# Three edits to the opening of a spectral filter with a low-rank mixer: order of table loads, packed f16 transposes, and the slots of one load

## The chip, the cores and the metric

The kernel runs on one core of one Trainium2 chip. The metric is the device time of one launch in microseconds (us), as the median of several runs. TensorE is called PE, VectorE DVE, ScalarE ACT, GpSimd POOL and SyncE SP, as in the profile; PEld is PE's weight load and a "q" behind an engine's name is its instruction queue.

## The reference

```python
X = np.fft.rfft(x, axis=1)                      # x: 8 x 3136 x 256, float32
Y = X * (filt_r + 1j * filt_i)[None]            # 1569 frequencies x 256
x = np.fft.irfft(Y, n=3136, axis=1)
h = x.transpose(0, 2, 1) @ U @ V                # U: 3136 x 32, V: 32 x 3136
u = x + h.transpose(0, 2, 1)
out = u + np.maximum(u @ w_ch1, 0) @ w_ch2      # w_ch1: 256 x 1024, w_ch2: 1024 x 256
```

Eight batches: a filter in the frequency domain along the sequence, a low-rank mixing along the sequence, and a two-layer network on each row.

## The kernel before

The Fourier transform of length 3136 is taken as 64 x 49, each half as matrix products. Frequencies come in 32 steps `s`. They are handled two at a time: index `m` runs from 0 to 15. Each step has its own table for the transform forward (`t2`) and back (`g12`), which are constants loaded from memory, and its own 256-wide rows of the filter (`ft`, real and imaginary). Tables and filter are loaded in four parts of eight steps, `PARTS = ((0, 8), (8, 16), (16, 24), (24, 32))`; in this text they are called part 0 to part 3, so part 1 covers `m` = 4 to 7. (The short name of the change counts from one.)

A part's filter is in use only after `swap_real` and `swap_imag` (DVE, lines 187 and 194) have copied it to the upper 64 partitions, the imaginary one with its sign turned.

Batch 0 goes a way of its own, without a round trip through memory:

- `first_f1` multiplies the four chunks of `x` with the 64-point matrix, one group of four rows `r0` after the other, and evicts the products in turns by ACT and DVE (L299, L301) into `at`. Matmuls named `keep` fill PE's gaps here. The loads of the tables are called from inside this loop. Each call first clears two columns of the destination on DVE (L156); the load on SP's queue (L157) waits for that, so a load leaves when DVE reaches the place in its order where the call stands.
- `first_a` (L321, L323) transposes two steps of `at` into the form in which the second transform reads them.
- `first_mid` is the loop over `m`. In turn `m` DVE multiplies spectrum and filter (`both_products`, L444, named `uv`), PE transforms the products of turn `m - 1` back (`back`, L340), the spectrum of turn `m + 2` forward (`forward`, L436, named `px`) and does one more `first_a`. ACT evicts what `back` gives (L343, named `et`). At the start of a new part DVE makes that part's swaps. Tables of parts 2 and 3 are called in turns `m` = 1 and 5. From turn 6 on, each turn takes one unit of batch 1's first transform (`fill`, from `f1_units`, L402 and L406/L408, named `pf` and `asb`), whose results go out to a buffer `c1` in memory (L412).
- Behind the loop stands the second turn of the data: 25 rows of `et`, each in two halves of 128 columns, are multiplied with the identity (L379, `pe`) and evicted to `e2` (L383 by ACT, L385 by DVE), two rows or 512 columns an eviction. `prep_u` (L263, L266, L268), three units of `fill` and one of `v_units` stand between them at fixed rows.
- Then `h1_unit(0)` (L503, L507) sums `e2` over the sequence, and the network's matmuls begin (L525, L530, L562, L584).

All other batches run interleaved with the network of the batch before, by an order written out by hand. A slot is half of a pair of matmul groups, 48 slots a batch; `put(slot, generator)` sets in which slot a step stands. `load_a` (L421) loads a quarter of the steps from `c1`, `stream` works on it (L436, L444 or L455/L457, L472, L476) and stores the result in `c2` (L478), and `load_e` (L428) reads it back turned. These three are issued from SP's queue, each waiting there for what it needs, so that one that waits holds up those behind it.

The pools decide little here: tag `m` has four PSUM banks of 2 KB a partition, tag `o` two, tag `a2` four buffers.

```python
for n0 in range(0, NH, 2):
    pt = bank("m", "pe")                  # 128 x 512 f32, one bank
    ...
    if n0 % 4:
        nc.scalar.copy(dst, pt[0:k, 0:w * DM])
    else:
        nc.vector.tensor_copy(dst, pt[0:k, 0:w * DM])
```

Of the kernel before, what the change touches and what calls it, by code (L numbers as in the profile page):

```python
# [9 lines left out]
F16 = mybir.dt.float16  # L10
# [6 lines left out]
DM = 256  # L17
RANK = 32
ESC = 16.0
NH = 25  # L20
# [66 lines left out]
def kernel(  # L87
# [11 lines left out]
    nc = tc.nc  # L99
# [5 lines left out]
    sel_d = nc.inline_tensor(sel_np, name="seld")  # L105
    t2_d = nc.inline_tensor(t2_np, name="t2d")
    g_d = nc.inline_tensor(g_np, name="gd")
# [6 lines left out]
    ps = ctx.enter_context(tc.tile_pool(name="ps", bufs=2, space=bass.MemoryType.PSUM))  # L114
    ctx.enter_context(tc.manual_schedule())
    BUFS = {"x": 1, "f": 1, "m": 4, "o": 2}

    def bank(tag, name):
        return ps.tile([128, 512], F32, tag=tag, bufs=BUFS[tag], name=name)
# [22 lines left out]
    idn = cst.tile([128, 128], F16)  # L142
    nc.sync.dma_start(idn, idn_d.ap())
    t2 = cst.tile([98, NS * 128], F16)
    g12 = cst.tile([128, NS * 2 * 98], F16)
    ft = cst.tile([128, 2 * NS * DM], F16)
    nyq = cst.tile([65, DM], F32)
    PARTS = ((0, 8), (8, 16), (16, 24), (24, 32))
# [1 line left out]
        for c in (0, NS * DM):  # L150
            nc.vector.memset(ft[32:64, c + a * DM:c + b * DM], 0.0)

    def load_tables(a, b):

        for dst, src, w in ((t2, t2_d, 128), (g12, g_d, 196)):
            nc.vector.memset(dst[:, a * w:a * w + 2], 0.0)  # L156
            nc.sync.dma_start(dst[:, a * w:b * w], src.ap()[:, a * w:b * w])  # L157

# [26 lines left out]
    def swap_real(a, b):  # L185

        nc.vector.tensor_copy(ft[64:128, a * DM:b * DM], ft[0:64, a * DM:b * DM])

    def swap_imag(a, b):

        fb = NS * DM
        if a == 0:
            nc.vector.memset(ft[0:1, fb:fb + DM], 0.0)
        nc.vector.tensor_scalar_mul(ft[64:128, fb + a * DM:fb + b * DM],
                                    ft[0:64, fb + a * DM:fb + b * DM], -1.0)
# [26 lines left out]
    sel = cst.tile([32, 128], F16)  # L222
# [52 lines left out]
    def first_f1():  # L275
        ne = 0
        keep = bank("x", "keep")
        xs = [st[0]["x"][c] for c in range(len(CH))]
        for r0 in range(0, NH - 1, 4):
            if r0 == 8:  # L280
                load_tables(*PARTS[0])
                nc.sync.dma_start(sel, sel_d.ap())
            if r0 == 20:
                load_tables(*PARTS[1])
            for dh in range(2):
                for k in range(4 if r0 < 16 else 0):
                    nc.tensor.matmul(keep[:, k * 128:(k + 1) * 128], w64[:, :], idn[:, :],
                                     start=True, stop=True, skip_group_check=True)
                pa = bank("m", "pa")
                for rr in range(4):  # L290
                    c = next(k for k in range(len(CH)) if r0 + rr < c0[k + 1])
                    o = (r0 + rr - c0[c]) * DM + dh * 128
                    nc.tensor.matmul(pa[:, rr * 128:(rr + 1) * 128], xs[c][:, o:o + 128], w64[:, :],
                                     start=True, stop=True, skip_group_check=True)
                for h in range(2):
                    dst = atv[:, dh, :, h * NH + r0:h * NH + r0 + 4]
                    src = pa.rearrange("p (r h k) -> p h k r", h=2, k=64)[:, h]
                    if ne % 2:
                        nc.vector.tensor_copy(dst, src)  # L299
                    else:  # L300
                        nc.scalar.copy(dst, src)  # L301
                    ne += 1
        pa = bank("m", "pa")
        o = (NH - 1 - c0[-2]) * DM
        for dh in range(2):
            nc.tensor.matmul(pa[:, dh * 64:(dh + 1) * 64],
                             xs[-1][0:64, o + dh * 128:o + (dh + 1) * 128], w64[0:64, 0:64],
                             start=True, stop=True, skip_group_check=True)
        nc.scalar.copy(atv[:, :, :, NH - 1],
                       pa[:, 0:128].rearrange("p (e k) -> p e k", e=2))  # L310
# [15 lines left out]
    def first_mid(fill):  # L326

        et = sb.tile([128, 2 * NH * 128], F16, tag="e2", bufs=2, name="et")
        etv = et.rearrange("p (e r h k) -> p h e r k", e=2, h=2, k=64)
        pend = None  # L330

        def back(m, uv):
            pi = bank("fx"[m % 2], "pi")
            for sl in range(2):
                for dh in range(2):
                    for fi in range(2):
                        g = (4 * m + 2 * sl + fi) * 98
                        o = fi * 512 + sl * DM + dh * 128
                        a = (dh * 2 + sl) * 98
                        nc.tensor.matmul(pi[:, a:a + 98], uv[:, o:o + 128], g12[:, g:g + 98],  # L340
                                         start=(fi == 0), stop=(fi == 1), skip_group_check=True)
            for h in range(2):
                nc.scalar.copy(  # L343
                    etv[:, h, :, 0:NH - h, 4 * m:4 * m + 4],
                    pi[:, 0:392].rearrange("p (e k r) -> p e r k", e=2, r=NR)
                    [:, :, h * NH:h * NH + NH - h])

        def ahead(m):
            return forward(m, st[0]["a"][m // 4], ("m",))

        pxs = [ahead(0), ahead(1)]
        for m in range(NS // 2):
            for k, part in enumerate(PARTS):
                if k and 2 * m == part[0]:
                    swap_real(*part)
                    swap_imag(*part)
            uv = both_products(m, pxs.pop(0))
            if pend is not None:
                back(*pend)
            pend = (m, uv)  # L360
            if m + 2 < NS // 2:
                pxs.append(ahead(m + 2))
            if m + 3 < NS // 2:
                first_a(m + 3)
            for k, part in enumerate(PARTS):
                if k > 1 and 2 * m + 14 == part[0]:
                    load_tables(*part)
            if m >= 6:
                next(fill)
        back(*pend)  # L370
        e2 = new_e2(0)
        for n0 in range(0, NH, 2):
            pt = bank("m", "pe")
            w = min(2, NH - n0)
            k = 64 if w == 1 else 128
            for rr in range(w):
                for dh in range(2):
                    o, a = rr * DM + dh * 128, (dh * NH + n0 + rr) * 128
                    nc.tensor.matmul(pt[0:k, o:o + 128], et[:, a:a + k], idn[:, :],  # L379
                                     start=True, stop=True, skip_group_check=True)  # L380
            dst = e2[0:k, n0 * DM:(n0 + w) * DM]
            if n0 % 4:
                nc.scalar.copy(dst, pt[0:k, 0:w * DM])  # L383
            else:
                nc.vector.tensor_copy(dst, pt[0:k, 0:w * DM])  # L385
            if n0 == 6:
                prep_u()
            if n0 in (10, 14, 18):
                next(fill)
            if n0 == 22:  # L390
                next(vgen)

    def f1_units(b, both):
# [37 lines left out]
    def forward(m, a2, xtags):  # L431
        ml = m % (KG // 2)
        px = bank(xtags[m % len(xtags)], "px")
        for sl in range(2):
            s = 2 * m + sl
            nc.tensor.matmul(px[:, sl * DM:(sl + 1) * DM], t2[:, s * 128:(s + 1) * 128],  # L436
                             a2[:, (2 * ml + sl) * DM:(2 * ml + sl + 1) * DM],
                             start=True, stop=True, skip_group_check=True)
        return px
# [54 lines left out]
    def one(load, b, k):  # L494
        load(b, k)
        yield
# [108 lines left out]
    def put(slot, gen):  # L605
        sched.setdefault(int(slot + 0.5), []).append(gen)
# [8 lines left out]
    SB = 48  # L615

    first_f1()
    swap_real(*PARTS[0])
    swap_imag(*PARTS[0])
    nc.vector.tensor_copy(ft[64:65, 0:DM], nyq[64:65, :])  # L620
    for m in range(3):
        first_a(m)
# [16 lines left out]
    for k, t in enumerate(steps):  # L639
        put(t, mid)  # L640
        b, m = divmod(k - LAG, NP)
        if k >= LAG and m % GP == GP - 1:
            put(t + (4 if b else 3), one(load_e, b + 1, m // GP))
    for b in range(1, nb):
        for gi in range(NS // KG):
            t = steps[NP * (b - 1) + GP * gi]
            put(t - (6 if b == 1 else 8), one(load_a, b, gi))
        put(SB * b - 4, h1_unit(b))
        if b > 1:
            fill = f1_units(b, b == 2)  # L650
            for k in range(NF):
                put(4 + 1.1 * k if b == 2 else steps[NP * (b - 1)] - 49 + 3 * k, fill)
            for c in range(len(CH)):
                if b > 2:
                    put(steps[NP * (b - 1)] - 68 + 10 * c, one(load_x, b, c))
# [53 lines left out]
```

## Time and profile before

| | |
|---|---|
| median of 3 runs | 558.92 us (558.39 to 560.25) |
| profiled execution | 560.77 us, span of its instructions 559.0 us |
| PE busy | 528.6 us, 95% of the span |
| DVE, ACT, POOL busy | 367.9, 363.6, 243.4 us |
| idle PE before 75 us | 21 us of the 75 |
| mean granted clock of PE | 0.989 |

The span is shorter than the time of its execution by 1.77 us, which lie ahead of the first and behind the last instruction. Rows of the timeline give the start, the duration, the engine with the line, and in brackets how long the engine had been idle and what ended that. Rows of the waits give the time in total, the number of waits and the longest. PE is busy nearly without a gap from 75 us to the last few us; what the change touches lies ahead of that.

### The profile page before, as it was taken

The numbers are of one execution on the slowest core, as the hardware profiler recorded it, in microseconds if no ns is written. First come the engines' busy times: TensorE is split into PE (matmuls) and PEld (weight loads), VectorE is DVE, ScalarE is ACT, GpSimd is POOL, SyncE is SP. The second block draws the span as 40 slices with busy tenths as digits, with TensorE's granted clock in tenths as the row PEclk, the third lists the DMA queues.
The fourth block names the chain that finished last, engine by engine and source line by source line (L and its number), as shares of the span: only waits on it lengthen the run. The fifth ranks groups of instructions, "written<-read, shape, count | busy, mean of one in ns | idle before, by whom it ended". The sixth has DMA issues, their size and how long they took to land.

```text
span 559.0 us, 11594 instructions
## 1 busy us (share of the span) xinstructions
PE 528.6 (95%) x4442; PEld 377.2 (67%) x4442; DVE 367.9 (66%) x541; ACT 363.6 (65%) x735; POOL 243.4 (44%) x349
## 2 busy tenths in 40 slices
PE   4577899999999999999999999999999999999996
PEld 4455467767677767677676766777677767767665
DVE  7696276757777577767777577767777587424342
ACT  3488765767767586777767586677666576654441
POOL 7457241255546455555546465555444344210000
PEclk9699999999999999999999999999999999999999
DMA  8999969877978757787868747786757535631233
GB/s 132 193 214 232 203 149 215 157 184 167 203 186 201 186 142 158 176 202 178 209 168 200 185 129 165 178 209 167 178 155 160 136 96 111 140 84 43 72 76 86
DMA packets 68170, 89.83 MB, mean 161 GB/s; under 512 B 6714, under 2 KB 53339, under 8 KB 67219
## 3 DMA queue, kind: packets, MB, share of 16 engines
q0 software_dynamic: 18512, 48.00, 40.0%
q1 hardware_dynamic: 49522, 41.03, 30.6%
q8 instruction: 35, 0.57, 0.5%
q14 instruction: 21, 0.16, 0.1%
q10 hardware_dynamic: 80, 0.07, 0.0%
HBM read 56.80 MB, written 48.17 MB: 188 GB/s over the span
## 4 chain that ended last, share of the span: by engine, by line
PE 81%; DMA 9%; DVE 4%; ACT 3%; issue 1%; POOL 0%; ACTq 0%; DVEq 0%; POOLq 0%
PE po L584 30%; PE phh L562 28%; PE pi L472 5%; PE px L436 4%; PE po L588 4%; PE pu L525 4%; PE pu L530 3%; DMA a<-c 3%; PE pf L402 2%; DMA xt<-in_x_dram 2%; DMA ft<-in_filt_i_dram 2%; DMA t<-t2d 1%; DVE uv L457 1%; PE ph L503 1%; ACT h L569 1%
## 5 line engine op out<-in xcount | busy, mean ns | idle before, releaser
L569 ACT ACTIVATE h<-phh 128x512 f16<-128x512 f32 (+1 forms) x350 | 186.3, 576 | 105.7 <-PE phh L562 105.7
L584 PE MATMUL po<-w,h 128*128 128x256 f16 x1568 | 203.2, 273 | 0.0
L562 PE MATMUL phh<-ut,w 128*128 128x512 f16 x768 | 197.5, 379 | 0.4 <-ACT ut L555 0.2
L460 POOL TENSOR_TENSOR y<-uv 128x512 f16<-128x512 f16 x96 | 110.3, 1149 | 149.4 <-DVE uv L457 74.7
L584 PEld LDWEIGHTS <-h 128*128 128x128 f16 x1568 | 150.1, 98 | 35.8
L457 DVE TENSOR_TENSOR uv<-px,ft 64x512 f16<-64x512 f32 x192 | 132.1, 688 | 2.6
L593 DVE COPY och<-po 128x512 f32<-128x512 f32 x96 | 66.4, 692 | 79.7 <-PE po L588 78.3
L562 PEld LDWEIGHTS <-w 128*128 128x128 f16 x832 | 74.5, 97 | 52.7 <-issue 3.2
L455 DVE TENSOR_TENSOR uv<-px,ft 128x512 f16<-128x512 f32 x96 | 66.0, 688 | 54.7 <-PE px L436 52.7
L476 ACT CAST esb<-pi 98x512 f16<-98x512 f32 x112 | 65.7, 587 | 39.9 <-PE pi L472 32.1
L601 POOL DMA_DIRECT2D out_dram<-och x84 | 45.6, 546 | 64.0 <-DVE och L593 64.0
L408 ACT CAST asb<-pf 128x512 f16<-128x512 f32 (+1 forms) x84 | 48.6, 578 | 14.8 <-PE pf L402 14.8
L436 PE MATMUL px<-a,t 98*128 98x256 f16 x256 | 49.9, 278 | 6.8 <-DMA a<-c 2.0
L567 DVE TENSOR_SCALAR h<-phh 128x512 f16<-128x512 f32 (+1 forms) x66 | 42.9, 649 | 18.9 <-PE phh L562 18.4
L555 ACT CAST ut<-pu 128x512 f16<-128x512 f32 x96 | 51.8, 598 | 2.2 <-PE pu L530 1.9
L588 PE MATMUL po<-idn,ut 128*128 128x128 f16 x384 | 52.8, 219 | 0.0
L444 DVE TENSOR_TENSOR uv<-px,ft 128x1024 f16<-128x1024 f32 x32 | 38.1, 1220 | 12.4 <-PE px L436 11.9
L530 PEld LDWEIGHTS <-e 128*128 128x128 f16 (+1 forms) x400 | 30.9, 97 | 17.6 <-issue 2.3
L525 PE MATMUL pu<-vr,h 128*128 128x512 f16 (+1 forms) x112 | 39.6, 354 | 1.3 <-ACT h L507 0.5
L588 PEld LDWEIGHTS <-ut 128*128 128x128 f16 x384 | 37.6, 98 | 4.4
L530 PE MATMUL pu<-s,e 128*128 128x128 f16 (+1 forms) x400 | 40.3, 218 | 0.0
L436 PEld LDWEIGHTS <-t 98*128 98x128 f16 x256 | 22.5, 100 | 24.7 <-issue 6.8
(73 smaller groups left out, 370.9 us busy)
## 6 DMA issues: line engine op xcount, KB each, us to landing
out_dram<-och POOLq DMA_DIRECT2D x84, 256.0 KB, 4.1
a<-c SPq DMA_DIRECT2D x28, 392.0 KB
c<-esb SPq DMA_DIRECT2D x28, 392.0 KB
xt<-in_x_dram POOLq DMA_DIRECT2D x56, 192.0 KB, 5.4
c<-asb POOLq DMA_DIRECT2D x42, 192.0 KB, 3.2
e<-c SPq DMA_DIRECT2D x28, 200.0 KB
e<-c SPq DMA_DIRECT2D x28, 192.0 KB
out_dram<-och SPq DMA_DIRECT2D x12, 256.0 KB
```

The costliest lines, as they stand in the source:

```text
L436: nc.tensor.matmul(px[:, sl * DM:(sl + 1) * DM], t2[:, s * 128:(s + 1) * 128], a2[:, (2 * ml + sl) * DM:(2 * ml + sl + 1) * DM], start=Tru ...
L455: nc.vector.tensor_mul(uv[:, 0:512], px[:, :], ft[:, a:a + 512])
L457: nc.vector.tensor_mul(uv[p:p + 64, 512:1024], px[q:q + 64, :], ft[q:q + 64, b:b + 512])
L460: nc.gpsimd.tensor_add(y, uv[:, 0:512], uv[:, 512:1024])
L476: nc.scalar.copy(esb[:, ml * 512:(ml + 1) * 512], pi[0:98, :])
L525: nc.tensor.matmul(pm[:, o:o + nr * k], h1[:, dh * 128:(dh + 1) * 128], vr[:, r0 * 128:r0 * 128 + nr * k], start=True, stop=False, skip_gr ...
L530: nc.tensor.matmul(pm[:, o + rr * k:o + (rr + 1) * k], e2[0:k, a:a + 128], s2[0:k, 0:k], start=False, stop=(rr == nr - 1), skip_group_chec ...
L562: nc.tensor.matmul(pm[:, 0:w], w1[:, dh * 1024 + t * 128:dh * 1024 + (t + 1) * 128], ut[:, dh * w:(dh + 1) * w], start=(dh == 0), stop=(dh ...
L569: nc.scalar.activation(h[:, 0:w], pm[:, 0:w], RELU)
L584: nc.tensor.matmul(po[:, o:o + DM], hs[gx, t][:, rr * 128:(rr + 1) * 128], w2[:, t * DM:(t + 1) * DM], start=(t == 0), stop=False, skip_gr ...
L588: nc.tensor.matmul(po[:, o + dh * 128:o + (dh + 1) * 128], ut[:, dh * w + rr * 128:dh * w + (rr + 1) * 128], idn[:, :], start=False, stop= ...
L593: nc.vector.tensor_copy(och[:, a:(rr + 1) * DM], po[:, 0:(rr + 1) * DM - a])
```

## The change

1. The tables of part 0 are no longer called together at `r0 == 8` but one by one: `t2` at `r0 == 4`, `g12` at `r0 == 16`. The tables of part 1, called before at `r0 == 20`, and the small constant `sel` are called behind part 0's `swap_imag`, ahead of the copy of `nyq`.
2. The second turn of batch 0 uses PE's transposes into f16 tiles of 128 x 1024 in PSUM (the same 2 KB a partition). Four rows make one eviction: seven evictions, of which ACT makes the second, the fifth and the last, which has one row, and DVE the other four, in place of thirteen.
3. `load_a` stands nine slots ahead of its use, in place of six (batch 1) or eight (the others).

On PE and POOL the order of instructions stays as it was. On SP it differs at four places: part 1's tables stand ahead of `sel` and no longer behind it; the last load of batch 1 stands ahead of the first pair of `load_e` and no longer behind it; the second and the third load of batch 2 each stand ahead of a store to `c2` (the last of batch 1, the first of batch 2) that they stood behind.

```diff
-    def load_tables(a, b):
-        for dst, src, w in ((t2, t2_d, 128), (g12, g_d, 196)):
+    def load_tables(a, b, which=(0, 1)):
+        for k in which:
+            dst, src, w = ((t2, t2_d, 128), (g12, g_d, 196))[k]
             nc.vector.memset(dst[:, a * w:a * w + 2], 0.0)
             nc.sync.dma_start(dst[:, a * w:b * w], src.ap()[:, a * w:b * w])
...
         for r0 in range(0, NH - 1, 4):
-            if r0 == 8:
-                load_tables(*PARTS[0])
-                nc.sync.dma_start(sel, sel_d.ap())
-            if r0 == 20:
-                load_tables(*PARTS[1])
+            if r0 in (4, 16):
+                load_tables(*PARTS[0], which=(r0 // 16,))
...
-        for n0 in range(0, NH, 2):
-            pt = bank("m", "pe")
-            w = min(2, NH - n0)
+        for k4, n0 in enumerate(range(0, NH, 4)):
+            pt = ps.tile([128, 1024], F16, tag="m", bufs=BUFS["m"], name="pe")
+            w = min(4, NH - n0)
...
-                    nc.tensor.matmul(pt[0:k, o:o + 128], et[:, a:a + k], idn[:, :],
-                                     start=True, stop=True, skip_group_check=True)
+                    nc.tensor.transpose(pt[0:k, o:o + 128], et[:, a:a + k], idn[:, :])
...
-            if n0 % 4:
-                nc.scalar.copy(dst, pt[0:k, 0:w * DM])
-            else:
-                nc.vector.tensor_copy(dst, pt[0:k, 0:w * DM])
-            if n0 == 6:
+            (nc.scalar.copy if k4 in (1, 4, 6) else nc.vector.tensor_copy)(dst, pt[0:k, 0:w * DM])
+            if k4 == 1:
                 prep_u()
-            if n0 in (10, 14, 18):
+            if k4 in (2, 3, 4):
                 next(fill)
-            if n0 == 22:
+            if k4 == 5:
                 next(vgen)
...
     first_f1()
     swap_real(*PARTS[0])
     swap_imag(*PARTS[0])
+    load_tables(*PARTS[1])
+    nc.sync.dma_start(sel, sel_d.ap())
     nc.vector.tensor_copy(ft[64:65, 0:DM], nyq[64:65, :])
...
-            put(t - (6 if b == 1 else 8), one(load_a, b, gi))
+            put(t - 9, one(load_a, b, gi))
```

## The prediction

> **What bounds the kernel now.** I read the page first, then the busy time by stretches, the waits, the chain that ended last and the timeline of the first 75 us. The page's strips are forty slices of 14 us:
>
> ```profile
> PE   4577899999999999999999999999999999999996
> ...
> PEclk9699999999999999999999999999999999999999
> ```
>
> From the sixth slice on TensorE is full, so only what moves the end of the opening, or fills one of PE's few gaps behind it, moves the time. By stretches (us, busy with counts, clock, DMA share, GB/s):
>
> ```profile
> 15.00:30.00 15.00, 9.00 (x89) 7.46 (x87) 10.20 (x20) 7.75 (x20) 7.48 (x13) 0.66 1.09 192
> 30.00:45.00 15.00, 11.82 (x145) 8.79 (x144) 14.73 (x17) 13.17 (x38) 6.24 (x11) 1.00 1.13 228
> 45.00:60.00 15.00, 12.44 (x129) 7.22 (x130) 6.87 (x13) 12.38 (x30) 12.68 (x22) 1.00 1.10 220
> 60.00:75.00 15.00, 13.09 (x91) 7.53 (x89) 7.45 (x9) 10.38 (x22) 3.19 (x6) 1.00 0.94 187
> ```
>
> The fourth column of busy times is ACT's, the third DVE's: from 30 to 45 us DVE is busy 14.73 of 15, so the loop over `m` runs at DVE's pace once it has begun, with ACT close behind. The DMA engines are full throughout (share about 1), so a load that is put off leaves its place to another. The timeline shows where DVE begins and who waits for tables:
>
> ```profile
> 12.36 0.38 SPq L157 DMA_DIRECT2D g<-gd  x1
> ...
> 16.46 0.32 SPq L157 DMA_DIRECT2D t<-t2d  x1
> ...
> 22.26 0.69 DVE L194 TENSOR_SCALAR ft<-ft 64x2048 f16<-64x2048 f16 x1 [4.12 <-DMA ft<-in_filt_i_dram]
> ...
> 25.77 0.32 SPq L157 DMA_DIRECT2D t<-t2d  x1
> ...
> 32.79 0.39 PE L436 MATMUL px<-a,t 98*128 98x256 f16 x2 [0.36 <-DMA t<-t2d]
> ```
>
> DVE stood still for 4.12 us until part 0's imaginary filter was in. From 22.26 it runs on without a gap of note to the last product at 46.23. Two pieces of the chain tell the rest:
>
> ```profile
> 31.89 7.62 DMA t<-t2d
> ...
> 58.55 8.22 DMA a<-c
> ```
>
> The load of batch 1's first quarter starts when `c1` is written (the last `asb` leave DVE and ACT at 51.96 and 52.13, their stores land at 58.3) and lands at 66.8. PE then waits for it:
>
> ```profile
> PE px L436 <- DMA a<-c: 1.4, 1, 1.4
> PE ph L503 <- ACT esb L476: 0.8, 1, 0.8
> ```
>
> So the end follows: part 0's filter, DVE's loop, the `asb` evictions, store, load at 66.8. The second row (at 120.94) is named in the third edit.
>
> **Edit 1, the tables.** In the landing records the last engine finished the imaginary filter's first piece (L163) at 17.23 and the second (L166) at 22.16; part 0's `g12` was in at 21.64. The same second piece of the real filter took 0.55 us longer than the one ahead of it (15.32, 15.87). What lies between 17.23 and 22.16 is then mostly the tables' traffic. Part 0's `t2` now leaves at about 10.5 (behind the first two copies on DVE, which end at 10.43) and not at 12.01; `g12` leaves at about 15.4 (its clear stands behind the copy of 14.84) and not at 12.36. Its first packets came 3.5 us behind the issue, so they come at about 18.9. The filter's piece then ends near 17.23 + 0.55 + about 1.1 for the share of `t2` that is now ahead of it = 18.9: **3.3 us earlier**. The floor is DVE itself (copies to 17.18, L187 0.69, L193 0.17: 18.05, gain 4.2); the other end is 0.5, if the filter still shares its engines with `g12`. `g12` itself lands near 22 instead of 21.64 and is needed by `back(0)` at about 22: no cost, up to 0.5 if it is a us later. The earlier `t2` meets the last chunk of `x` (14.66) and may delay it by up to 0.8; DVE's copies then end at 18.0, still ahead of the filter.
>
> Against that stands a new wait. Part 1's `t2` left at 16.46, during the stall; now it leaves 0.8 us after `swap_imag` starts (0.69, two clears, 0.09 to SP). From issue to the first use of such a table took 6.9 us (12.01 to 18.92), 7.0 (25.77 to 32.79) and 7.6 (31.89 to 39.51) where PE waited for it; I take 7.0. `px` of `m` = 4 takes up to 0.6 and DVE starts that product 8.4 us after `swap_imag` began; before, it was 29.48 - 22.26 = 7.22. So **1.2 us are lost** (0 at a latency of 5.8, 3.2 at the 9.0 that part 1's `g12` took from 16.82 to 25.84). Queued behind the waiting `px` on PE are `first_a`, `back(2)` and the next `px`. With PE at half clock a turn took 1.48 and 1.66 (starts of `back`: 24.65, 26.13, 27.79), DVE's product takes 1.2: three turns would lose 1.0, at full clock none. The granted clock was half from 17.5 to 27.75, and PE will idle again before the table lands; I take **0.5**. The tables of part 2 stand behind part 1's on SP; they landed at 32.7 with 2.3 us to spare before DVE needed them, which covers a delay of that size. `sel` is first used at 52: nothing. Edit 1: -3.3 + 1.2 + 0.5 = **-1.6**.
>
> **Edit 2, the transposes.** PE's fifty matmuls stay fifty of the same width: nothing. The stretch is paced by ACT:
>
> ```profile
> 48.11 1.07 ACT L383 CAST e<-pe 128x512 f16<-128x512 f32 x2 [0.71 <-PE pe L379]
> ...
> 49.07 0.88 ACT L266 CAST usb<-pu 128x512 f16<-128x512 f32 x2
> ...
> 49.98 0.18 DVE L268 CAST usb<-pu 64x32 f16<-64x32 f32 x1 [0.81 <-ACT usb L266]
> 50.09 1.27 DVE L385 CAST e<-pe 128x512 f16<-128x512 f32 x2
> ...
> 51.29 0.67 DVE L406 CAST asb<-pf 128x512 f16<-128x512 f32 x1
> ...
> 51.73 0.40 ACT L408 CAST asb<-pf 64x256 f16<-64x256 f32 x1
> ```
>
> ACT gives up six evictions of 0.53 (3.2 us) for two of 1024 columns and a small one: 0.576 for 512 and 0.38 for 256 make 0.77 ns a column, so 0.97 each and 0.4: 2.3. But its first can start only after four rows, 0.5 later, so `usb` and DVE's L268 behind it slip by 0.4, and ACT's second big one stands ahead of the last `asb`, which goes from 52.13 to about 52.9. On DVE an eviction of 1024 f16 columns from PSUM is in no row: above it stands twice 0.64 = 1.28 (f32 from PSUM), below it 0.35 (half of L187's 0.69, f16 in SBUF). With 0.35 DVE's `asb` ends at about 51.8, with 1.28 at 53.6. The nearest row is the read of PSUM, with the saved fixed part 1.1: 53.3. The store then leaves 0.8 to 1.5 later; the engines are full with batch 2's `x` until 62.5, so a late store partly finds what it would have waited for. I take **+0.4** at the load of 66.8, bounds -0.3 and +1.5. `h1_unit(0)` moves by -0.3 to +0.9, covered by the 1.4 us that PE waits there.
>
> By the Trainium skill (VectorE: DVE Perf Modes, "The perf-mode tier table") a copy out of PSUM runs at up to two elements a cycle if both ends are 16 bit; with its rate this eviction would be estimated at 0.65 us and DVE's `asb` would end at 52.4. A rule there speaks against the edit: "TensorE: Matmul & The Clock Gate", Part 4, says that transposes don't count as busy PE for the clock as matmuls do. If so the clock, 1.00 from 27.75 on in this trace, could drop at about 51 and make the network's first matmuls slow, at most 1.7 us for one window, most of it inside the wait for the load; the sum with it would be 0.3 to 1 us longer.
>
> **Edit 3, the loads.** Batch 1's first three loads stand behind the same store of `c1` as before: nothing. Its last no longer waits for a store to land (it left at 85.67, could leave at 82.0), but PE had no wait for it. The load at 110.78 went out right behind the store of 110.41 and ran beside it; that store landed 4.4 us later, one with nothing behind it took 3.1 (81.67 to 84.84), another 4.9. Put ahead of it, the load is done before and the two `load_e` behind the store come earlier, for which PE waited 0.8 at 120.94: **-0.5** (0 to -0.8).
>
> **Sum:** -1.6 + 0.4 - 0.5 = -1.7 us on the profiled 560.77, 559.07. That execution lies 1.85 above the median of the runs, so I forecast 558.92 - 1.7 = **557.2**.
>
> **Rivals.** *A wash:* the filter comes 1 to 2.5 us earlier and the table's wait gives it back: 1.2 + 0.5 + 0.4 - 0.5 less that is +0.6 to -0.9, **558.0 to 559.5**. For it: each term of the sum has the size of its bounds. *Slower:* the place is `px` of `m` = 4, where PE stands in order for part 1's `t2`. It decides once the latency exceeds 5.8 us by more than the filter has gained. With the 8.4 us midway to 9.0, a gain of 1.5, a cold PE for three turns and edit 2's upper half: 2.6 - 1.5 + 1.0 + 0.9 - 0.5 = +2.5, **561.4**. For it: full DMA engines and a half clock; against: rows of 7. *Not what it says:* the evictions of 1024 columns cost twice those of 512, then edit 2 alone is +0.9 to +1.5 and the sum -0.9 (inside the wash).
>
> **Numbers.** A measurement of this kernel tells about 0.3% from no change, 1.7 us: 557.2 to 560.6. The forecast sits at that edge, its own range is 555.0 to 557.2 (floor: filter at 18.05, latency 6, the 0.8 of edit 3). Forecast 0.41, wash 0.33, slower 0.26. The range is 555.0 to 561.3, leaving out a tenth at each end.
>
> **What would show it.** Right: L194 starts at 18.7 to 20, PE waits for `t<-t2d` at `m` = 4 for 1 to 3 us, the first L436 of batch 1 comes at 65 to 66, L503's wait near 120 is under 0.4. Wrong: L194 not before 21, a wait of over 3 us at that `px`, DVE's eviction of 1024 columns above 1.1 us, or a clock of half behind 45 us.

## The result, and the profile after

The changed kernel takes 562.54 us (median of 20 runs, 559.43 to 565.31). Before, in 20 runs between them, it is 559.50 (557.78 to 562.86). The ratio is 1.0042, 95% interval 1.0025 to 1.0060: slower by about 2.4 us. The forecast was 557.2, and its range ended at 561.3.

The profiled execution of the changed kernel took 560.48 us (span 558.7), 2.06 under its own median, while that of before took 560.77, 1.27 over the 559.50 given here and 1.85 over the median of the three runs known when the forecast was made. The two traces are thus nearly of one length, and their difference isn't the effect. What an edit does was read from 17 traces and from the timed runs of 15 more kernels.

The page's strips, PE's busy tenths and its granted clock, slices of 14 us:

```profile
PE   4587899999999999999999999999999999999996
...
PEclk9689999999999999999999999999999999999999
```

In slices of this width the picture behind 75 us is the same as before. Still, not all that the change touches lies ahead of 75 us: the loads that edit 3 moves stand between 80 and 145 us. The third slice of the clock is 8, not 9. Busy time by stretches of the changed kernel (PE, PEld, DVE, ACT, POOL, then clock, DMA share, GB/s):

```profile
15.00:30.00 15.00, 8.67 (x78) 7.25 (x77) 11.77 (x22) 7.28 (x18) 7.41 (x14) 0.62 1.10 213
30.00:45.00 15.00, 13.00 (x154) 10.15 (x152) 13.85 (x15) 13.84 (x41) 6.25 (x10) 0.93 1.09 212
45.00:60.00 15.00, 12.54 (x128) 7.05 (x127) 4.68 (x9) 11.46 (x26) 12.66 (x22) 1.00 1.11 214
60.00:75.00 15.00, 12.89 (x85) 7.26 (x83) 7.45 (x9) 10.18 (x22) 3.21 (x6) 1.00 0.85 185
```

In the first stretch DVE has done more (11.77 us against 10.20), since its filter came sooner. In the second it has done less (13.85 against 14.73): it has lost its gapless run. In the third DVE is busy 2.2 us less than before (4.68 against 6.87), ACT only 0.9 less (11.46 against 12.38). The timeline shows the start of DVE's loop and the new wait:

```profile
18.32 0.69 DVE L195 TENSOR_SCALAR ft<-ft 64x2048 f16<-64x2048 f16 x1 [0.17 <-DMA ft<-in_filt_i_dram]
19.14 0.31 SPq L158 DMA_DIRECT2D t<-t2d  x1
...
26.41 0.61 PE L430 MATMUL px<-a,t 98*128 98x256 f16 x2 [2.47 <-DMA t<-t2d]
...
27.06 1.23 DVE L438 TENSOR_TENSOR uv<-px,ft 128x1024 f16<-128x1024 f32 x1 [1.50 <-PE px L430]
```

`swap_imag` starts at 18.32, not 22.26. Part 1's `t2` leaves at 19.14 and lands 7.2 us later. PE stands 2.47 us for it, and DVE 1.50 behind PE. Each of the next three products waits another 0.42 to 0.46 us for PE, whose granted clock is half until 32.1 us. The loop's last product ends at 45.47, only 0.8 earlier than before. Then the second turn, in the same view:

```profile
47.35 0.69 DVE L379 COPY e<-pe 128x1024 f16<-128x1024 f16 x1 [1.64 <-PE pe L377]
47.80 1.01 ACT L379 COPY e<-pe 128x1024 f16<-128x1024 f16 x1 [1.16 <-PE pe L377]
...
49.71 1.27 DVE L379 COPY e<-pe 128x1024 f16<-128x1024 f16 x2
...
50.87 1.01 ACT L379 COPY e<-pe 128x1024 f16<-128x1024 f16 x1 [0.52 <-PE pe L377]
50.91 0.67 DVE L400 CAST asb<-pf 128x512 f16<-128x512 f32 x1
...
51.78 0.37 ACT L402 CAST asb<-pf 64x256 f16<-64x256 f32 x1
```

An eviction of 1024 f16 columns takes DVE 0.67 to 0.69 us (1.27 for two in a row) and ACT 1.01. ACT's second one, at 50.87, stands directly ahead of its last `asb`, which ends at 52.15; DVE's `asb` has been done since 51.58. So it is ACT's `asb` that sends the store of `c1`, as before, but by 0.57 us and no longer by 0.17. What was won by 45.47 is used up: before, ACT's last `asb` ended at 52.13. The chain that ended last has behind it

```profile
58.82 7.61 DMA a<-c
```

(before it left at 58.55), and of PE's waits (total, times, longest) up to 140 us these carry the new ones:

```profile
PE px L430 <- DMA t<-t2d: 2.5, 1, 2.5
PE px L430 <- DMA a<-c: 2.3, 2, 1.6
...
PE ph L497 <- ACT esb L470: 0.7, 1, 0.7
```

### The profile page after: what moved, and what is told of

Its sections match the earlier page's. It is cut to its first block, busy times and chain, and to the rows that moved or that the text cites. A ratio compares the mean times of both kernels' runs of the same rounds, so it can differ in the third digit from the quotient of the medians.

```text
span 558.7 us, 11589 instructions
## 1 busy us (share of the span) xinstructions
PE 529.1 (95%) x4442; PEld 377.7 (68%) x4442; DVE 366.5 (66%) x538; ACT 363.3 (65%) x732; POOL 244.4 (44%) x349
## 4 chain that ended last, share of the span: by engine, by line
PE 83%; DMA 7%; ACT 4%; DVE 3%; issue 1%; POOL 1%; ACTq 0%; DVEq 0%; POOLq 0%
PE po L578 30%; PE phh L556 28%; PE px L430 5%; PE pi L466 5%; PE po L582 4%; PE pu L519 4%; PE pu L524 3%; DMA a<-c 3%; PE pf L396 2%; DVE uv L451 1%; DMA t<-t2d 1%; PE ph L497 1%; DMA ft<-in_filt_i_dram 1%; ACT h L563 1%; DMA xt<-in_x_dram 1%
```

## The experiments

Four explanations of the loss were set against each other. **T**: part 1's tables, late behind the swap, make PE and DVE wait. **E**: the fifth eviction (`k4 == 4`) on ACT stands ahead of ACT's last `asb`, so the load of batch 1 leaves later. **Q**: the loads put earlier stand ahead of a store in SP's queue, which lands later, so the `load_e` behind it is later. **C**: transposes don't hold PE's clock. In the first four expectations V stands for E and C together, and L for loads that share the DMA engines with stores and with `load_e`. Medians and ratios stand beside runs of the kernel before made between them; one kernel has 12 timed runs. Executions of one kernel scatter by 1.2 to 2.8 us (standard deviation), so a single ratio is uncertain by 0.3%, and the joint fit at the end of this section does the weighing.

**One edit alone, and two without the tables.** Each is the kernel before with the named hunks of the diff. *tables_only* (edit 1):

> Edit 1 alone (the table loads). Theory T (tables): the filter comes 4 us earlier, but TensorE stands at the px of m = 4 for part 1's t2 and the half clock lasts past 32 us, so the loop is no earlier or later in most runs: 1.003 to 1.006 of before. Theory V (evictions): the opening keeps what the trace of the changed kernel shows, 0.998 to 1.000. Theory L (loads): the same as V.

*transposes_only* (edit 2):

> Edit 2 alone (f16 transposes, 1024 columns an eviction). Theory V: usb and the asb behind the large ACT eviction are late, c1 is stored 0.7 to 1.5 us later, and transposes let the clock fall in some runs: 1.002 to 1.005. Theories T and L: 0.999 to 1.001; the evictions are not what sets the load of batch 1.

*loads_only* (edit 3):

> Edit 3 alone (load_a nine slots ahead). Theory L: the moved loads share the DMA engines with load_e and with the stores, so e2 or a later quarter comes late: 1.002 to 1.005. Theories T and V: 0.999 to 1.000, and the wait of the h1 matmuls near 120 us is 0.8 or less.

*no_tables* (edits 2 and 3):

> Edits 2 and 3 without edit 1. Theory T: 0.998 to 1.001, all of the loss gone. Theory V or L: 1.003 to 1.006, all of the loss still there. Additive: the product of the two single ones.

Measured: 559.18, 561.37, 561.09 and 562.45 us; ratios 0.9983 (0.9952 to 1.0014), 1.0016 (0.9990 to 1.0042), 1.0028 (0.9995 to 1.0062) and 1.0035 (1.0009 to 1.0062). T falls: without the tables nearly the whole loss is there, and the tables alone lose nothing. Edits 2 and 3 both lean to slower.

The trace of loads_only holds a reading that matters for edit 1. Its tables are called as in the kernel before, and still:

```profile
18.80 0.69 DVE L194 TENSOR_SCALAR ft<-ft 64x2048 f16<-64x2048 f16 x1 [1.40 <-DMA ft<-in_filt_i_dram]
```

The prediction took 22.26 from one execution. Over ten traces without edit 1 this start lies between 18.80 and 22.26, mean 20.90, and 22.26 is the latest of all. With edit 1 it lies between 18.23 and 19.70 in seven traces, mean 18.78.

**What of edit 2 costs.** *transposes_512* keeps thirteen evictions and their engines as before and changes only the kind of the matmul and the PSUM type:

```diff
-            pt = bank("m", "pe")
+            pt = ps.tile([128, 512], F16, tag="m", bufs=BUFS["m"], name="pe")
...
-                    nc.tensor.matmul(pt[0:k, o:o + 128], et[:, a:a + k], idn[:, :],
-                                     start=True, stop=True, skip_group_check=True)
+                    nc.tensor.transpose(pt[0:k, o:o + 128], et[:, a:a + k], idn[:, :])
```

> f16 transposes, but 512 columns an eviction and the engines as before, thirteen evictions. Theory E (the loss of edit 2 is the order of the evictions: the last asb of ACT stands behind an eviction of 1 us): ACT's last asb comes 4.7 us or less behind the first transpose as in the kernel before (5.45 with edit 2), first px of batch 1 18.2 to 18.5 us behind it, 0.999 to 1.000. Theory C (transposes do not count for the clock): a half clock between 46 and 58 us and 1.001 to 1.003, with asb as late as with edit 2.

*transposes_dve* is edit 2 with the fifth eviction on DVE:

```diff
-            (nc.scalar.copy if k4 in (1, 4, 6) else nc.vector.tensor_copy)(dst, pt[0:k, 0:w * DM])
+            (nc.scalar.copy if k4 in (1, 6) else nc.vector.tensor_copy)(dst, pt[0:k, 0:w * DM])
```

> Edit 2 with the fifth eviction on DVE in place of ACT, so that ACT's last asb stands behind nothing. Theory E: that asb comes 4.7 us or less behind the first transpose, the load of batch 1 is issued at most 11.0 behind it (12.0 with edit 2), 0.998 to 1.000. Theory C: no change against edit 2 alone, 1.001 to 1.003.

Measured: 559.28 us, ratio 0.9996 (0.9968 to 1.0025), and 559.23, ratio 0.9985 (0.9958 to 1.0012), the same transposes as in transposes_only at 561.37. The timeline of transposes_dve:

```profile
50.54 0.67 DVE L402 CAST asb<-pf 128x512 f16<-128x512 f32 x1
50.72 0.37 ACT L404 CAST asb<-pf 64x256 f16<-64x256 f32 x1 [0.75 <-PE pf L398]
```

ACT now waits for PE ahead of its last `asb`, not behind an eviction. From the first transpose (46.32) to the end of that `asb` it is 4.77 us, as without edit 2 (4.67 to 4.68). In the changed kernel, transposes_only, no_tables and tables_and_transposes it is 5.45 to 5.46, and in all four PE then waits 1.3 to 1.7 us for the load of `a`. In transposes_dve it doesn't wait for it. That wait isn't the eviction's alone, and the traces don't settle the path from the `asb` to the loss. The kernel before waits 1.4 and loads_batch2 1.0, both without edit 2; of the kernels told below that have the eviction on DVE, changed_fifth_dve and best_of_all wait 1.7 and 2.9. By the semaphore records of the 17 traces the load itself takes anything from 4.1 to 10.7 us, which is far more than the 0.8 us at stake. That the place of this one eviction costs time is shown by the stretch and by the timed runs; that it costs it through the load is likely, but argued.

*transposes_act_twice* gives ACT the sixth eviction as well:

```diff
-            (nc.scalar.copy if k4 in (1, 4, 6) else nc.vector.tensor_copy)(dst, pt[0:k, 0:w * DM])
+            (nc.scalar.copy if k4 in (1, 4, 5, 6) else nc.vector.tensor_copy)(dst, pt[0:k, 0:w * DM])
```

> Edit 2 alone with the sixth eviction on ACT as well as the fifth, so that two of 1.01 us stand ahead of ACT's last asb. Theory E (the last asb sets the store, the load of batch 1 and the start of the stream): from the first transpose to ACT's last asb 6.0 to 6.5 us (5.45 with edit 2, 4.67 before), PE's wait for the load 2.2 to 2.7 us in place of 1.3 to 1.7, median 0.5 to 1 above that of edit 2 alone (561.4). Rival (edit 2 costs for another reason, such as the matmuls' kind): the stretch longer, the median as edit 2 alone.

Measured: 561.32 us, ratio 1.0024 (0.9999 to 1.0049). The expectation misread the order: the last unit of `fill` stands behind the fifth eviction, so the sixth comes behind the last `asb`, and that `asb` ended 5.45 us after the first transpose, as in edit 2 alone. The network began 0.9 us later for it (first `phh` 9.20 us after the first transpose, against 8.29), PE's wait for the load was gone, and the time was that of edit 2 alone. In this trace the load left 10.6 us after the first transpose, and not at about 12 as in the four kernels above, although the `asb` was as late: the store of `c1` landed sooner. So the sixth eviction adds nothing to the time. That its microsecond is absorbed by the wait for the load would explain this, but one trace in which the load was early doesn't show it.

**What of edit 3 costs.** *loads_batch1* and *loads_batch2* move one half of the loads:

```diff
-            put(t - (6 if b == 1 else 8), one(load_a, b, gi))
+            put(t - (9 if b == 1 else 8), one(load_a, b, gi))      # loads_batch1
+            put(t - (6 if b == 1 else 9), one(load_a, b, gi))      # loads_batch2
```

> Edit 3 for batch 1 alone: its last load stands ahead of the first pair of load_e. Theory Q (a load put ahead of a store on SP's queue makes the store land later, and load_e and the h1 matmuls with it): there is no store behind the moved load, so 0.999 to 1.001, and the wait of the h1 matmuls near 120 us is 0.8 or less. Rival (the load delays the first pair of load_e): 1.001 to 1.003.

> Edit 3 for the batches from 2 on alone: two loads stand ahead of the stores they stood behind. Theory Q: the store of about 110 us lands 4.2 to 6.4 us behind its issue (3.2 to 4.4 without the edit), h1 near 120 waits 0.7 to 2.3, 1.001 to 1.004. Rival: 0.999 to 1.001.

Measured: 559.49 us, ratio 0.9972 (0.9941 to 1.0004), and 560.96, ratio 1.0014 (0.9986 to 1.0043). Only batch 2's loads lean to slower. In the timeline of SP's queue the one of them in question stands, in loads_only, ahead of batch 1's last store to `c2`:

```profile
103.69 0.67 SPq L421 DMA_DIRECT2D a<-c  x1
107.58 0.33 SPq L478 DMA_DIRECT2D c<-esb  x1
113.97 1.17 SPq L428 DMA_DIRECT2D e<-c  x2
...
119.64 0.92 PE L503 MATMUL ph<-e,usb 128*32 128x256 f16 x25 [2.32 <-DMA e<-c]
```

and behind it in tables_only, where the loads are as before:

```profile
108.12 0.33 SPq L476 DMA_DIRECT2D c<-esb  x1
108.50 0.52 SPq L419 DMA_DIRECT2D a<-c  x1
111.73 0.78 SPq L426 DMA_DIRECT2D e<-c  x2
...
118.54 0.93 PE L501 MATMUL ph<-e,usb 128*32 128x256 f16 x25 [0.67 <-ACT esb L474]
```

From the store's issue to that of `load_e`, which waits for it, it is 6.4 us in the first and 3.6 in the second. Over the six traces that have the moved load and the store on SP's queue the mean is 5.1 (4.2 to 6.4), over nine without the moved load 3.9 (3.4 to 4.4).

Was it the place in the queue? *loads_act_store* is edit 3 with that one store issued from ACT's queue, where no load stands ahead of it. *fifth_dve_act_store* does this in the whole change with the fifth eviction on DVE:

```diff
-                nc.sync.dma_start(spec(c2[b], gi), ...)
+                (nc.scalar if (b, gi) == (1, 3) else nc.sync).dma_start(spec(c2[b], gi), ...)
```

> Edit 3 alone, but batch 1's last store to c2 is issued from ACT's queue and so stands behind no load on SP's. Theory Q (the order in the queue is what costs): from that store's issue to the issue of the load_e behind it 3.5 to 4.4 us as without the moved load (mean 3.9 in eight traces), PE's wait at h1 of batch 1 0.7, median within 0.5 of the kernel before. Rival, sharing (the packets of the moved load take the engines whatever the queue): 4.9 to 6.4 us as in the six traces with the moved load, the wait 0.7 to 2.4, median 1 to 1.5 above before.

> The whole change with the fifth eviction on DVE and batch 1's last store to c2 on ACT's queue. If edits 2 and 3 cost by the ACT eviction and the queue alone, what is left is edit 1's gain of 0.7 and that of a shorter second turn: 1 to 1.5 below before, as best_of_all (ratio 0.997). If the loads cost by sharing the engines, it stays level with before as changed_fifth_dve did (ratio 0.9998).

Measured: 561.82 us, ratio 1.0039 (1.0012 to 1.0067), and 560.35, ratio 1.0031 (1.0001 to 1.0060). Neither came back. The timeline of fifth_dve_act_store:

```profile
108.63 0.60 ACTq L472 DMA_DIRECT2D c<-esb  x1
113.75 1.04 SPq L422 DMA_DIRECT2D e<-c  x2
...
120.14 0.92 PE L497 MATMUL ph<-e,usb 128*32 128x256 f16 x25 [1.78 <-DMA e<-c]
```

On a queue of its own the store still needs 5.1 us here, and PE still waits 1.78. The trace of loads_act_store, its fastest run, shows 4.2 and 0.67, as Q had it, while its median is what sharing had. The landings decide between the two. In loads_only the moved load lands at 112.75, long after the store was issued at 107.58, and the store lands at 113.95. In all eight traces with batch 2's loads moved the load is still on its way when this store is issued, and the store lands 1.1 to 1.8 us behind it, whichever queue issued it (1.8 in loads_act_store, 1.2 in fifth_dve_act_store). The other moved load is a control: it stands ahead of a store near 142 us too, but has landed by the time that store is issued, and there the `load_e` leaves 3.0 to 3.6 us after the store, against 3.3 to 3.6 in the nine traces without the edit. So it is not the place in the queue; what goes with the delay in every trace is a load that is still in flight. The Trainium skill (DMA: Bandwidth & Descriptors, "Issuing engines are not separate DMA queues") says that transfers started by different engines run on the same 16 DMA engines and interleave there, and that starting them on several saves only the time of issuing; these two runs fit that.

**Pairs, and the change mended.** *tables_and_transposes* (edits 1 and 2) and *tables_and_loads* (edits 1 and 3):

> Edits 1 and 2 without edit 3. Theory E (the main loss is the fifth eviction on ACT ahead of the last asb): 1.000 to 1.003, ACT's last asb 5.45 us behind the first transpose and a wait of PE for the load of batch 1 of 1.3 to 1.7. Theory Q (the main loss is the two loads ahead of stores): 0.997 to 1.000.

> Edits 1 and 3 without edit 2. Theory E: 0.998 to 1.001, ACT's last asb 4.7 us behind the first transpose and no wait for the load of batch 1 over 1 us. Theory Q: 1.001 to 1.004. In both the filter's swap starts at 18.3 to 19.5 us and PE waits 1.5 to 3 us for part 1's table.

*changed_fifth_dve* is the whole change with the fifth eviction on DVE. *best_of_all* is that, with only batch 1's loads moved (the two short diffs above):

> The whole change with one thing undone: the fifth eviction is DVE's, not ACT's. Theory E: about 0.002 below the changed kernel, 1.000 to 1.003 of before; ACT's last asb 4.8 us behind the first transpose, load issued 10.1 to 10.9 behind it. Theory Q: as the changed kernel, 1.003 to 1.006.

> Edit 1, edit 2 with the fifth eviction on DVE, edit 3 for batch 1 alone. Theories E and Q: 0.995 to 0.999; each of the three was at or below 1 by itself. If the parts work against each other: 1.000 to 1.003.

Measured: 561.19 us, ratio 1.0010 (0.9984 to 1.0036); 561.00, 0.9995 (0.9973 to 1.0017); 560.48, 0.9998 (0.9967 to 1.0029); 559.47, 0.9970 (0.9947 to 0.9994). The first two lie in the range that E gave and outside Q's, but their intervals reach into both. In changed_fifth_dve the load was issued 11.25 us behind the first transpose, later than expected. The last beats both kernels, the one before by 0.3%; its interval ends just under 1.

**The joint fit.** Least squares over the 277 timed runs of before, of the changed kernel and of the eleven others that are made of whole edits or of the variants in the table (without transposes_512, transposes_act_twice and the two with a store on ACT's queue), with one level for each set of runs made together (effect in us, standard error):

| part | effect |
|---|---|
| edit 1 | -0.6 (0.35) |
| edit 2 as written | +1.35 (0.33) |
| edit 2, fifth eviction on DVE | -0.5 (0.4) |
| edit 3, batch 1's load | +0.1 (0.4) |
| edit 3, batch 2's loads | +1.1 (0.4) |

The first, second, fourth and fifth row sum to +1.9 for the changed kernel; the means of its runs and of those beside them differ by 2.4. Two rows are clear of zero by more than twice their error, edit 2 as written and batch 2's loads; so is the difference between the two rows of edit 2, 1.9 (0.46). The fit takes the parts as adding up, which no run tests by itself.

## Why the prediction was wrong

The changed kernel is slower, where -1.7 us was forecast. Between that and the fit's +1.9, edit 3 makes about 1.7 of the difference, edits 1 and 2 about 1.0 each. None of the four signs named for "wrong" came. Of those for "right" the two on edit 1 came nearly as said; the first L436 of batch 1 (66.46, where 65 to 66 was said) and the wait at `h1` (0.7, under 0.4 was said) did not. By the sum's own terms:

**Edit 1, forecast -1.6: the sign right, the gain of the filter too large.** `swap_imag` came where it was forecast, or a little earlier (18.32; 18.7 to 20 was said). The latency of part 1's `t2` was 7.2 (7.0), DVE's stall 1.50 (1.2). From the swap's start to the last product the loop takes 26.2 us in the mean of seven traces with edit 1 and 24.7 in ten without: 1.5 lost, where 1.2 + 0.5 was forecast. The failed term is the 3.3. It was measured from 22.26, the latest start of ten; from their mean of 20.90 the gain is 2.1. 2.1 - 1.5 is 0.6, which is what the fit gives. The text knew that its execution lay 1.85 above the median, and subtracted this from the total only: it was not asked whether the stall to be removed was part of the excess.

Two things in the loop were priced too low or not at all. Part 0's `g12`, for which "no cost" was forecast, is what PE's first `back` waits for in all seven traces with edit 1 (PE idle 1.1 to 4.2 us ahead of it) and in none of the ten without; in tables_and_transposes DVE lost 1.4 us behind it. And an early loop meets the filter of a later part: of the 17 traces seven show DVE waiting 0.3 to 1.0 us for it at 37 to 40 us, all with the swap's start before 20.9 us, and the six with a later start show no such wait. So not all of the 1.5 is the wait for part 1's `t2`.

**Edit 2, forecast +0.4 with bounds -0.3 to +1.5: right in kind, taken too low.** The step "from 52.13 to about 52.9" for ACT's last `asb` was right, +0.77 from the first transpose on. On DVE 1.1 us was taken for an eviction that takes 0.67 to 0.69, so DVE, forecast as the last, was not the last. The estimate of 0.65 worked out from the Trainium skill's page (VectorE: DVE Perf Modes, "The perf-mode tier table") was right, and the choice by the nearest row was wrong. What failed is the discount behind it, "a late store partly finds what it would have waited for": the load of `a` left 11.7 to 12.3 us after the first transpose in the four kernels with the eviction on ACT, 10.1 in transposes_dve, and PE waited for it in each of the four. In transposes_act_twice it left after 10.6, and in the eight traces without the large evictions after 9.9 to 11.9 (mean 10.7). The fit gives +1.35, inside the bounds. How the loss runs from the late `asb` to the end is open, as said above.

**The rule on transposes and the clock** (the Trainium skill, TensorE: Matmul & The Clock Gate, Part 4) is not seen. In the changed kernel the clock is 1.00 from 45 to 75 us. Of ten traces with transposes nine have no half clock between the first transpose and 60 us; the tenth (transposes_act_twice, at 57.5) has other waits of PE ahead of it. And the same transposes with one eviction moved cost nothing. The fifty transposes take 3.8 us of a stretch of 5.5 that also holds matmuls; a longer run of transposes alone was not tried.

**Edit 3, forecast -0.5: the wrong sign.** The step that failed is "Put ahead of it, the load is done before". The load left SP at 103.69 in loads_only and the store at 107.58, but the load was not done: it landed at 112.75, and the store behind it. The wait of `h1` near 120 us grew: 1.3 us in the mean of eight traces with batch 2's loads moved, 0.8 in nine without. The row of 0.8 on which the gain was built was also misread: it names ACT's `esb` as what came last, so the `load_e` were not what PE waited for, and there was no 0.8 to gain. About half of the +1.1 is seen at this wait. Where the rest lies is open. In tables_and_loads a wait of 2.37 there is followed by a half clock, in the view by stretches:

```profile
120.00:125.00 5.00, 5.00 (x37) 3.26 (x30) 0.00 (x0) 1.82 (x4) 0.76 (x1) 0.50 0.04 7
```

In loads_only two later waits at `h1` (1.53 and 1.44 us) are longer than elsewhere although the order there is that of before. Moving the load ahead of the store of about 110 us by still more slots, so that it lands before that store is issued, was not tried.

**The rivals.** The slower one had its number near (561.4 against 562.5) but not its mechanism: it put the loss at `px` of `m` = 4, and the tables alone don't lose, so that its number came near by luck. The one on evictions, "the evictions of 1024 columns cost twice those of 512", nearly holds on ACT (1.01 against 0.53 to 0.63) but not on DVE, and its +0.9 to +1.5 for edit 2 is what came; it was put inside the wash because edit 1 was to pay for it.

## What to carry to other kernels

Before a stall is priced, see whether it has its usual length: here the start that the change was to bring forward was the latest of ten traces. When several evictions are merged into larger ones, look at which short instruction stands behind the larger one on its engine and who waits for that; here one eviction moved to the other engine turned +1.35 us into -0.5. A load put earlier runs beside other transfers; a store that is issued while it is still in flight landed behind it in every trace here, and another issuing queue did not bring the time back. A load that had landed before its store was issued cost that store nothing.

## What the hardware showed that was not expected

A granted half clock comes in pieces of 3.41 us: where they end inside the span, half-clock stretches of the 17 traces lasted 3.41, 6.83, 10.24 or 13.65 us. Their number differs between executions of one kernel. The Trainium skill (TensorE: Matmul & The Clock Gate, Part 1, "The HAM clock gate") gives a free-running window of this length; the traces agree on the length, and no run here shows whether the window runs free. Over the timed runs one more microsecond of half clock goes with about a quarter of a microsecond of time, which makes up about a fifth of the variance that the fit leaves; edit 1 adds 1.3 (standard error 0.7) us of it, about 0.3 us of time, where 0.5 was forecast for "a cold PE".

ACT gained nothing to speak of from f16 in PSUM: an eviction of 512 columns took it 0.53 to 0.63 us in transposes_512 and with f32 before, while on DVE it took 0.37 to 0.44 us (0.64 before), each counted from rows of the timeline with one eviction or two in a row.
